# Linear attention and a gated convolution FFN on one core: unread matmuls at the start, k^T v copied between halves by DMA, and another written-out order

## The chip, the core and the metric

The kernel runs on one core of a Trainium2 chip. The metric is the device time in microseconds. An engine here is one of PE (matmul; PEld is its weight loads), DVE (vector), ACT (scalar, with its function tables), POOL and SP; each works through its own list of instructions in order and waits where an operand isn't ready. SP only issues DMAs here, POOL issues the loads and does a little arithmetic.

## The reference

Inputs are q, k, v of 8 batches, 8 heads, 576 positions and 64 columns, a gain of 64, and the FFN's weights. For each batch and head:

```
kv  = k^T v                                   # 64 x 64
o   = q kv                                    # 576 x 64
x   = o / sqrt(mean(o*o) + 1e-6) * g_norm     # heads side by side: 576 x 512
h   = relu(x w_in)                            # 576 x 1024
c   = conv over positions, 3 taps per column of h
out = (h * sigmoid(c)) w_out                  # 576 x 512, f32
```

## The kernel before

The eight batches go through in five groups: 0, 1, (2,3), (4,5), (6,7). Heads are handled in pairs; a pair is a t of 0 to 3, its two heads on partitions 0 to 63 and 64 to 127. The 576 positions are split in two halves of 288, called e.

For each batch, POOL loads k, v and q (line 239) as bf16, from f32 in DRAM; two buffers each. Batch 0 comes in two parts, of six and two heads. PE then does:

- kv_mm (line 380): k^T v. Group 0 (KV_TWICE 1) computes each product twice, so that it stands in both partition halves. The other groups compute it once, and kv_out (lines 386 to 397) copies each head's result into both halves, in four evictions of 64x256.
- tr_mm (line 430): transposes q through PE; tr_out evicts qT.
- out_mm (product, line 353): o from kv and qT, into a PSUM tile of two banks (a ring of three). ACT squares it (line 453), and for groups 0 to 2 "keep" stores it times g_norm in o32. Groups 3 and 4 ("dma") compute the product again later (out_again).
- ss_mm (line 507): sums of squares. ln_exp on ACT makes rs, the reciprocal root (lines 518, 519); group 4 uses a Newton iteration on POOL instead (lines 534 to 537).
- rs is then spread over partitions: by matmul (rb_mm, lines 624 and 627) in groups 0 to 2, after a split into bf16 parts on DVE from group 1 on; by DMA in groups 3 and 4. There "scatter" writes rs to DRAM (scr) and issues eight broadcast reads into rb (line 587), one entry in the order.
- x_mul or x_scale (lines 642, 648) on DVE gives xT.
- h_mm (line 746), eight matmuls for one f of 128 columns, and h_out with relu on ACT or DVE.
- The convolution: in group 0 on PE with diagonal weights (line 785), elsewhere on DVE: tap and add (lines 810, 831, 833). ACT does the sigmoid (lines 794, 837), DVE the gate (line 842).
- o_mm (line 698) with w_out, its eviction to o_sb (lines 333, 335; three buffers), and the store on SP (line 712). tails_mm takes the last 64 rows of two batches together.

A PSUM ring of two single banks serves k^T v, q's transposes, the sums and o_ps.

The order on all engines is written out: ORDER is a list of operation numbers, in which a letter a or d chooses ACT or DVE where both can do it, and "*n" puts n unread matmuls of 288 columns ("fill", line 343) ahead of that operation on PE, into the PSUM tile that it is about to write. The numbers count the plan.op calls. The costs, lat and dma figures given to plan.op are kept beside each operation and change nothing in the program: only ORDER and the data's own dependences do.

Of the kernel before, what the change touches and what calls it, by code (L numbers as in the profile page):

```python
# [25 lines left out]
def _patch_pnc_remap() -> None:  # L26
# [45 lines left out]
KV_TWICE = (1, 0, 0, 0, 0)  # L72
# [4 lines left out]
    0 105 11 104 8 10 12 1 2 7 17 18a 9 19 20d 29 30a 24 25d 26*5 27 21 22 6 34 35d 31 32 103 23a 36  # L77
    37d 41*7 28d 38*3 40d 33d 4 42 43*6 44 108 109d 39 49 45 46 5 50 3 13 118*9 123 124a 51 53 119a
    106 107a 54 204 47 110*5 111 113 114a 52 48 55 125 112d 56a 126 127d 14 203 202 68 69d 120 122d
    210 211d 121 220 115 116 59 117d 60d 128 129 130 57 58 77 64 207 215 65a 78a 73 74a 221d 131 132  # L80
    61 216d 62 225 226a 133 134 137 208 209a 138 206 135 82 136 83d 205 66 67 212 213 217 232 218
    364 214d 219d 233d 247 139 140a 222 224d 223 248d 227 237 238a 143 144a 242 243d 147 149 63 141
    75 228 142a 148 230 231d 362 79 229a 76 80 81 145 146a 363 15 234 249 250 236d 370 251a 70 239*4
    16 235 71 150 151 367 240 152 371d 153 155 86*3 87a 378 382 366 383d 244 245 156 365 72 379d 167
    252 168d 241d 253 254 374*2 375d 246a 84*3 85 163 164a 169 170a 88 165 154 89 255 157 158 166a
    171 90 259 256 368 369a 173 260 172 160 91 265 175 266 372 373 92d 93 267 268 174 376 377 388
    389a 384 385 396 397a 176 261*2 269 159 100 101a 161 179 516 515 270 262 177 257 386 380 97 387a
    381 390 392 258 178 283 180 393a 391 514 181 185 98d 400 401d 263 394 395 182 183 162 522 523d
    94 264 402 403 526 527d 184 519 398 271 399 95d 99 534 535a 520 521a 186 199 272d 284d 404 405
    285 286d 200a 277 273 278d 274d 287 275 276d 540 548 279 541a 290 549a 280d 518 281 552 528 282a  # L90
    529 517 536 537 538 539a 288 317 318a 309 313 314a 289 310a 291 292 294 293 96 311 312a 305 306a
    295 296 544 545a 550 551 303 304a 102 297 406 315 316a 307 308a 323 546 553d 554 555 547 319 321
    322 530 531a 190 191a 192 542 320 543 524 525 324 328 325 532 533 193 194a 407 408 409 410 556
    557 558 559 413 411 414 196 415 412 416 417 421 422 300 298 301 187 299 419 418 201 420 423 437
    424a 197a 438a 429 430a 431 425 432a 327 326 329 302 195 332 427 198 426a 439 428a 433 434a 441
    440 435 560 436a 442 443 444 445 447 446 331 333 461 462a 465 459 466a 448 460a 330 334 463 455
    456a 467 468a 469 188a 470a 457 458a 189 449 356 357a 358 464a 450 350 351a 352 453 359 360a 361
    563 561 573 471 474 473 341 342a 343 472 475 476 562 574 564 452 335 336a 344 345a 353 354a 480
    477 479 478 481 565 567 568 571 572 566 337 347 338 451 575 576 485 482 569 570 484 577 578a 454
    603 604a 483 486 585 579 580a 586 583 584a 588 607 629 348a 630a 581 582a 601 602a 587 346 511  # L100
    349 512a 608a 355 589 339a 590 591 592 593 605 606a 627 594 595 628a 599 597 625 609 663 496 631
    340 610 613 612 611 614 616 618 664a 598 626a 632a 617 490 497a 615 596 491a 513 498 619 622 620
    505 506a 507 600 633 634 492 636 635 649 651 508 652a 623 637 638 642 640 621 509a 510 641 502
    650a 503a 639 643 647 645 646 624 499 500a 672 690 653 654 644 655 504 501 691a 692 656 658 657
    659 673a 648 493 494a 495 487 665 666 660 667 668 669 661 488a 662 674 675 489 676 677 678 684
    685a 670 671 679 681 682a 687 686 680 693 683 688a 689 694d 695 705 706a 707 696 697d 698 699
    700d 701 702 703a 704
# [6 lines left out]
class Ring:  # L114


    def __init__(self, bufs):
        self.free = bufs
# [12 lines left out]
class Op:  # L131
# [4 lines left out]
    def __init__(self, at, group, engines, cost, fn, args, deps, need, lead, dma, lat):  # L136
        self.at, self.group, self.engines, self.cost = at, group, engines, cost
        self.fn, self.args, self.lead, self.dma, self.lat = fn, args, lead, dma, lat
        self.kind = fn.__name__ if fn else ""
        self.shape = SHAPE.get(self.kind, "")  # L140
        self.deps = sorted({d.at for d in deps})
        self.need = sorted({d.at for d in need})
        self.takes, self.gives = [], []
        self.engine, self.fill = engines[0], 0
# [7 lines left out]
class Plan:  # L152
# [8 lines left out]
    LOADED = 14.4  # L161
# [4 lines left out]
    def op(self, engines, cost, fn, *args, deps=(), need=(), lead=None, dma=0.0, lat=0.0):  # L166
# [3 lines left out]
               max(cost) if lead is None else lead, dma, lat)  # L170
# [20 lines left out]
def kernel(  # L191
# [37 lines left out]
    nc.scalar.preload_act_table_set(NORM_TABLES)  # L229

# [60 lines left out]
    nc.vector.tensor_copy(spread, spread_ps)  # L291

# [46 lines left out]
    def fill(op, ps):  # L339

        for _ in range(op.fill):
            n = min(ps.shape[-1], 288)
            nc.tensor.matmul(ps[:, :n], ident, spread.rearrange("p c m -> p (c m)")[:, :n],  # L343
# [690 lines left out]
```

## Time and profile before

The median of 13 runs is 206.15 us (205.03 to 208.11).

| | |
|---|---|
| profiled execution, its own time | 205.56 us |
| its span in the trace | 203.8 us |
| PE busy, of it fills | 184.0 us, 49 fills |
| DVE, ACT, POOL busy | 156.6, 139.2, 39.9 us |
| first v lands, first k^T v starts | 9.06, 9.19 us |
| first h_ps starts | 28.9 us |
| first h_ps of group 2 starts | 77.7 us |
| last k of batch 7 lands | 95.3 us |
| last matmul group starts | 197.5 us |

Times in the profile are microseconds from the start of the span, or nanoseconds where it says so. A line of groups gives source line, engine, operation, out<-in, shapes and count, then busy time and mean nanoseconds of one, then the idle time just before and what ended it. A window's line gives the stretch, its length and how long each engine was busy in it (with the number of instructions), then the granted clock, the DMA share and GB/s. The chain gives start, duration and what the time went to, from the last instruction back.

### The profile page before, as it was taken

The page shows a single profiled execution, that of the slowest core. Times are in us where ns is not written, and L with a number is a line of the kernel's source. Part 1 is how long each engine was busy: PE and PEld are TensorE (multiplying, and loading weights), DVE is VectorE, ACT ScalarE, POOL GpSimd, SP SyncE. Part 2 cuts the span into 40 slices and gives each one's busy share as a digit, 9 for nine tenths or more (in the row PEclk, how much of TensorE's full clock was granted, in tenths as well). Part 3 has the DMA queues.
Part 4 walks back from the last instruction along what each step waited for, and adds up shares of the span by engine and source line. Part 5 has one row for each costly group of instructions (what it writes and reads, how often), then busy time and mean ns, then how long its engine had stood idle before and what let it go on. Part 6 is the DMA issues. An engine that isn't in the chain of part 4 may idle for free.

```text
span 203.8 us, 4614 instructions
## 1 busy us (share of the span) xinstructions
PE 184.0 (90%) x1854; PEld 116.3 (57%) x1866; DVE 156.6 (77%) x289; ACT 139.2 (68%) x223; POOL 39.9 (20%) x61
## 2 busy tenths in 40 slices
PE   1299998998999999998999997896999999999991
PEld 0276665776677555776764575652448665554440
DVE  2145956768899898578979999999959999998320
ACT  2036364887889899856788969974598598686311
POOL 7706022070220503001000996000000000000000
PEclk9999999999999999999999999999999999999999
DMA  4999999999999499997994110897510341455554
GB/s 50 201 203 202 205 205 203 204 201 203 208 203 203 55 220 206 153 229 151 218 202 117 45 51 29 182 219 219 156 51 3 103 105 51 124 136 156 153 129 130
DMA packets 31593, 31.01 MB, mean 152 GB/s; under 512 B 2108, under 2 KB 26964, under 8 KB 31572
## 3 DMA queue, kind: packets, MB, share of 16 engines
q0 software_dynamic: 20976, 16.25, 52.5%
q1 hardware_dynamic: 10596, 14.47, 28.3%
q8 instruction: 14, 0.23, 0.5%
q14 instruction: 7, 0.06, 0.1%
HBM read 37.24 MB, written 9.73 MB: 230 GB/s over the span
## 4 chain that ended last, share of the span: by engine, by line
PE 52%; DMA 18%; issue 10%; POOL 9%; ACT 5%; DVE 4%; SPq 0%; POOLq 0%; ACTq 0%; DVEq 0%
PE o_ps L698 19%; PE h_ps L746 16%; DMA k_sb<-in_k_dram 7%; DMA out_dram<-o_sb 4%; PE kv_ps L380 3%; DMA v_sb<-in_v_dram 3%; PE qT_ps L430 3%; POOL rs L537 2%; PE rb_ps L624 2%; DMA rb<-scr 2%; PE c_ps L785 2%; ACT sq L453 2%; PE ot_ps L353 2%; DVE o L337 2%; PE ot_ps L343 1%
## 5 line engine op out<-in xcount | busy, mean ns | idle before, releaser
L746 PE MATMUL h_ps<-xT,w_in_sb 128*128 128x288 bf16 x512 | 67.4, 286 | 2.2 <-ACT h L757 1.8
L698 PE MATMUL o_ps<-w_out_sb,h 128*128 128x512 bf16 x260 | 60.3, 380 | 2.2 <-ACT o_sb L333 1.7
L746 PEld LDWEIGHTS <-w_in_sb 128*128 128x128 bf16 x512 | 48.9, 98 | 16.5 <-issue 2.9
L698 PEld LDWEIGHTS <-h 128*128 128x128 bf16 x272 | 25.7, 98 | 32.0 <-issue 3.3
L757 ACT ACTIVATE h<-h_ps 128x576 bf16<-128x576 f32 x53 | 33.3, 650 | 9.2 <-PE h_ps L746 8.7
L837 ACT ACTIVATE conv<-conv,cw_rel 128x576 bf16<-128x576 bf16 (+1 forms) x40 | 37.0, 960 | 1.8 <-DVE conv L833 1.6
L810 DVE TENSOR_SCALAR tap<-h,cw_rel 128x576 bf16<-128x576 bf16 (+1 forms) x80 | 31.4, 434 | 2.9 <-ACT h L757 2.1
L333 ACT ACTIVATE o_sb<-o_ps 128x512 f32<-128x512 f32 x30 | 17.8, 593 | 19.5 <-PE o_ps L698 10.3
L453 ACT ACTIVATE sq<-ot_ps 128x576 bf16<-128x576 f32 x32 | 20.1, 652 | 7.1 <-DVE o L337 4.1
L822 POOL COPY conv<-h 128x4 bf16<-128x4 bf16 (+3 forms) x12 | 3.3, 277 | 102.0 <-ACT h L757 71.6
L833 DVE TENSOR_TENSOR conv<-conv,tap 128x1152 bf16<-128x1152 bf16 (+11 forms) x36 | 21.9, 663 | 1.1
L842 DVE TENSOR_TENSOR h<-h,conv 128x1152 bf16<-128x1152 bf16 (+3 forms) x16 | 21.9, 1367 | 1.1 <-ACT conv L837 1.0
L831 DVE TENSOR_TENSOR conv<-h,tap 128x1152 bf16<-128x1152 bf16 (+11 forms) x36 | 20.4, 621 | 0.4
L333 ACT ACTIVATE kv_sb<-kv_ps 64x256 bf16<-64x256 f32 (+1 forms) x25 | 9.6, 382 | 12.4 <-PE kv_ps L380 12.1
L335 DVE COPY qT<-qT_ps 128x576 bf16<-128x576 bf16 x18 | 8.1, 452 | 8.7 <-PE qT_ps L430 8.7
L648 DVE SCALAR_TENSOR_TENSOR xT<-ot_ps,g_sb,rb 128x576 bf16<-128x576 f32 x16 | 12.2, 811 | 2.7 <-PE ot_ps L353 2.3
L239 POOL DMA_DIRECT2D q_sb<-in_q_dram x9 | 6.9, 768 | 35.8 <-PE qT_ps L430 25.2
L642 DVE TENSOR_TENSOR xT<-o,rb_ps 128x576 bf16<-128x576 f32 x15 | 11.0, 749 | 3.7 <-PE rb_ps L627 2.3
L353 PE MATMUL ot_ps<-qT,kv_sb 64*64 64x288 bf16 x192 | 12.9, 309 | 1.0 <-DVE o L337 0.4
L380 PE MATMUL kv_ps<-v_sb,k_sb 96*64 96x64 bf16 x432 | 10.2, 207 | 3.8 <-DMA v_sb<-in_v_dram 3.1
L430 PE MATMUL qT_ps<-ident,q_sb 96*128 96x96 bf16 x192 | 13.5, 215 | 0.0
L337 DVE TENSOR_SCALAR o<-ot_ps,g_sb 128x576 f32<-128x576 f32 x12 | 9.6, 812 | 5.1 <-ACT sq L453 4.1
(73 smaller groups left out, 161.4 us busy)
## 6 DMA issues: line engine op xcount, KB each, us to landing
out_dram<-o_sb SPq DMA_DIRECT2D x24, 192.0 KB, 2.4
rb<-scr SPq DMA_DIRECT2D x16, 288.0 KB, 6.1
q_sb<-in_q_dram POOLq DMA_DIRECT2D x7, 576.0 KB, 7.6
v_sb<-in_v_dram POOLq DMA_DIRECT2D x7, 576.0 KB, 11.7
k_sb<-in_k_dram POOLq DMA_DIRECT2D x7, 576.0 KB, 14.3
out_dram<-o_sb SPq DMA_DIRECT2D x24, 128.0 KB, 2.4
out_dram<-o_sb SPq DMA_DIRECT2D x24, 64.0 KB, 2.0
w_in_sb<-in_moe_w_in_dram POOLq DMA_DIRECT2D x2, 512.0 KB, 14.5
```

The source lines that it names most:

```text
L333: nc.scalar.activation(dst, src, AX.Copy, scale=1.0 if scale is None else scale)
L353: nc.tensor.matmul(ps[i * D:(i + 1) * D, e, :HS], g.kv[bi][es, t, i, :], g.qT[bi][es, 2 * t + i, :], start=True, stop=True)
L430: nc.tensor.transpose(ps[:, i, j * PS:(j + 1) * PS], q_sb[:, 2 * t + i, j * P:(j + 1) * P], ident[:PS, :PS])
L453: nc.scalar.activation(g.sq[bi, t], ust["ps"][:, :, :HS], AX.Square)
L698: nc.tensor.matmul(st["ps"][:n, :], g.h[:, f, t0:t0 + n], w_out_sb[:, f, :], start=(f == 0), stop=(f == n_ff - 1))
L746: nc.tensor.matmul(ps[:, e, :HS], w_in_sb[:, t, f * P:(f + 1) * P], g.xT[:, t, at:at + HS], start=(t == 0), stop=(t == n_hd - 1))
L757: nc.scalar.activation(dst, st["ps"][:, :, :HS], AX.Relu)
L810: eng.tensor_scalar_mul(cst["t"][:, f - f0, :], g.h[:, f, lo:lo + T], cw_rel[:, j, f:f + 1])
L831: nc.vector.tensor_add(c[:, :, here], h[:, :, here], t[:, :, there])
L833: nc.vector.tensor_add(c[:, :, there], c[:, :, there], t[:, :, here])
L837: nc.scalar.activation(cst["c"][:, f - f0, :], cst["c"][:, f - f0, :], AX.Sigmoid, scale=cw_rel[:, 1, f:f + 1])
L842: nc.vector.tensor_mul(hs, hs, cst["c"])
```

## The change

Five things change.

1. A tile of ones is set on DVE at the start, and PE runs 14 unread matmuls of it ahead of the transposes that make spread, and 22 after them. The fills ahead of single operations read ones too (instead of ident and spread), and there are 70 of them, not 49.
2. Groups 1 to 4 evict k^T v once, as 128x256, and kv_swap on SP copies it between the partition halves with two SBUF to SBUF DMAs of 32 KB. product reads slot 0 of kv for heads that are already in the right half and slot 1 for the swapped ones.
3. scatter is split: the write of scr, and four gathers of two broadcast reads each, which may stand apart in the order.
4. ORDER is another list: other positions on all engines, other choices of ACT and DVE, other loads first (v and k of batch 1, w_in, then q).
5. The planner's figures and its after and mates fields change (lat, LOADED); they act only through ORDER. tap can run on ACT by the code, but TAPS stays DVE.

The diff, without the list and the planner's figures:

```diff
-KV_TWICE = (1, 0, 0, 0, 0)
+KV_FROM = ("twice", "swap", "swap", "swap", "swap")
...
+    ones = consts.tile([P, 288], BF16, name="ones")
+    nc.vector.memset(ones, 1.0)
+    warm_ps = ps_one.tile([P, 288], FP32, name="warm_ps", tag="one")
+
+    def warm(n):
+        for _ in range(n):
+            nc.tensor.matmul(warm_ps, ones[:, :P], ones, start=True, stop=True)
+
+    warm(14)
...
     spread = consts.tile([P, 4, P], BF16, name="spread")
     nc.vector.tensor_copy(spread, spread_ps)
+    warm(22)
...
-            nc.tensor.matmul(ps[:, :n], ident, spread.rearrange("p c m -> p (c m)")[:, :n],
+            nc.tensor.matmul(ps[:, :n], ones[:, :P], ones[:, :n],
                              start=True, stop=True)
...
+                kv = (g.kv[bi][es, int(i != e), t, :] if g.kv_from == "swap"
+                      else g.kv[bi][es, t, i, :])
...
+                    if g.kv_from == "swap":
+                        g.kv[bi] = attn.tile([P, 2, n_hd, D], BF16, name="kv_sb", bufs=6)
+                        move(st["op"], g.kv[bi][:, 0, :, :], st["ps"][:, :, 0, :])
+                        return
...
+                def kv_swap(bi=bi):
+                    for i in range(2):
+                        nc.sync.dma_start(out=g.kv[bi][(1 - i) * D:(2 - i) * D, 1, :, :],
+                                          in_=g.kv[bi][i * D:(i + 1) * D, 0, :, :])
...
             def scatter():
-                scr = dram.tile([P, HS], FP32, name="scr")
-                nc.sync.dma_start(out=scr, in_=g.rs)
...
+                g.scr = dram.tile([P, HS], FP32, name="scr")
+                nc.sync.dma_start(out=g.scr, in_=g.rs)
+
+            def gather(t):
...
+                row = g.scr[t * SM:t * SM + 4 * g.G, :].rearrange("(c i) n -> i c n", i=2)
+                for i in range(2):
+                    nc.sync.dma_start(
+                        out=g.rb[i * D:(i + 1) * D, t, :, :],
+                        in_=row[i:i + 1].to_broadcast([D, 2 * g.G, HS]))
```

The start of the new order on PE reads, with the operations' names: k^T v of batch 0 (7 fills ahead), q's transposes t0 (8 fills) and t2, product t0, transposes t1, product t2, transposes t3 (3), product t1, k^T v of the last two heads, product t3 (3), sums, cw, rb t0 (6), sums (2), rb t2 (2), rb t1 (2), rb of t3's first half (2), k^T v of batch 1 (1), rb of t3's second half (1), h_mm f0 (1), f1, conv f0, h_mm f3, two transposes of batch 1. The first product of batch 1 follows conv f1. Group 1's and most of group 0's h_mm come ahead of q's transposes for group 2, where the old order mixed them.

## The prediction

> **What bounds it now.** I read the page's busy shares first, then the windows by stage, then the chain of waits in order of time. The first and second:
>
> ```profile
> PE 184.0 (90%) x1854; PEld 116.3 (57%) x1866; DVE 156.6 (77%) x289; ACT 139.2 (68%) x223; POOL 39.9 (20%) x61
> ...
> 28.90:67.30 38.40, 36.54 (x505) 26.84 (x501) 30.49 (x59) 30.20 (x50) 8.83 (x13) 1.00 1.29 202
> 67.30:77.70 10.40, 9.92 (x124) 4.95 (x122) 9.37 (x20) 9.22 (x18) 2.40 (x3) 1.00 0.92 147
> 110.00:142.80 32.80, 29.27 (x234) 18.32 (x230) 32.18 (x40) 25.84 (x34) 12.97 (x14) 1.00 0.54 129
> 142.80:197.50 54.70, 54.40 (x325) 29.76 (x331) 43.58 (x91) 38.11 (x58) 1.35 (x6) 1.00 0.39 107
> ```
>
> PE sets the time, but part of its 90% is no work: 49 filling matmuls, and at the start matmuls at half speed. From 142.8 us on PE has almost no gap. In 110 to 142.8 us DVE is busy 98% and PE stands 3.5 us. The chain shows the slow start and two later stalls:
>
> ```profile
> 2.23 6.82 DMA v_sb<-in_v_dram
> 9.06 0.14 issue
> 9.19 2.14 PE kv_ps L380 x72
> ...
> 13.11 1.20 PE ot_ps L343 x5
> ...
> 25.62 0.96 PE kv_ps L380 x48
> ...
> 27.75 0.72 PE ot_ps L343 x5
> ...
> 133.20 8.81 DMA out_dram<-o_sb
> 142.03 0.04 ACTq L333
> 142.07 0.05 issue
> 142.11 0.61 ACT o_sb L333
> ```
>
> The first k^T v takes 29.7 ns a matmul, the one at 25.62 us 20.0 ns; a fill takes 240 ns at 13.1 us, and 122 ns where fills stand among other warm work (288 columns; h_ps runs at 0.98 us for 8). The column of the granted clock says 1.00 all along, so the cold clock is read from durations alone. At 133 us a store lands 8.8 us later, behind the eight transfers that spread rs (rb<-scr), its o_sb comes free late, and PE stands 1.66 us at 141.1.
>
> Dividing each step's issue-to-issue time by its warm cost (h 0.99, o 1.73, product 0.25, transposes 0.26, k^T v 0.96 us), PE needs 169 us of own work and 6.0 us of fills after the first load (9.16 us); 15 us of waits and slow clock make up the rest up to the last o_ps at 197.5, and 6.3 us follow from its start on.
>
> **Part 1, warm matmuls and the first stage.** 14 fills start when ones is set, about 1.1 us (PE's first weight load stood at 1.26). At 240 ns they last to 4.5; the 16 transposes for spread need 0.6, then come 22 more. The rule in TensorE: Matmul & The Clock Gate, Part 1, is that some 3.4 us of sustained activity opens the clock, in a window that runs free of the kernel; that would open it at 4.5 to 8. The row here is slower: PE starts at 9.2 and reaches full speed only between 14.3 and 18, 5 to 9 us later, with gaps and transposes between. By the page the 22 end at about 8.2 and the 7 fills ahead of the first k^T v are over at the landing (9.06): nothing lost. By the row (open at 8) they end at 9.2 and the 7 at 10.1: 0.9 us lost. I take 0.5 late. If the clock didn't open at all, 22 + 7 at 240 ns would end at 12.1: 3 us lost.
>
> Walking the new order at warm costs: k^T v 9.6 to 11.0, 8 fills (1.0) to 12.0, transposes, first product 12.9 (before: 14.27). ACT then carries k^T v out 0.49, qT 0.65, three squares, keep 0.73 and the two rs steps 0.95, so the first rb_ps is at 17.1 (before: 19.63 after its fills). Four rb_ps pairs at 1.16 (one of them as two halves), 10 fills, and k^T v of batch 1 at 0.96 bring the first h_ps to 24.3 instead of 28.87. v and k of batch 1 are now loaded ahead of its q: k lands about 19.8 (now 22.75) and w_in 22.5 (now 25.3), so neither is late. Left over for afterwards are four transposes and one product of batch 1: 1.3 us. **-3.3 us.** The cover: diag (3 x 1.2 us on DVE) is now between the x steps; its last part ends at 25.7, and the first c_ps needs it at 26.3.
>
> **Part 2, k^T v by DMA.** Seven times, four evictions become one:
>
> ```profile
> L333 ACT ACTIVATE kv_sb<-kv_ps 64x256 bf16<-64x256 f32 x24 | 9.1, 378 | 3.1 <-PE kv_ps L380 2.7
> L335 DVE CAST kv_sb<-kv_ps 64x256 bf16<-64x256 f32 x4 | 1.7, 422 | 0.6 <-PE kv_ps L380 0.5
> L514 ACT ACT_TABLE_LOAD x2 | 2.6, 1283 | 0.0
> ```
>
> Of 28 pieces 7 stay: 10.8 us become about 2.7. ACT saves some 6.5, but the new order takes the sigmoid table before batch 1's rs and needs two more table loads (2.6), three more o_sb (1.8) and three more keeps (2.2): ACT stays as it is, DVE sheds 5. Neither sets the end, so this is worth nothing directly. What is added is a wait: kv_mm, eviction (0.39 and 0.2 of hops), then two DMAs of 32 KB on SP, then the product. PE work between a k^T v and its batch's first product in the new order: batch 1 5.8 us, batch 2 12.4, batch 3 6.0, batch 4 17, batch 5 9.3, batch 6 8.0, batch 7 5.3. The nearest rows of SP's transfers, with loads in flight (83 to 97 us) and without:
>
> ```profile
> out_dram<-o_sb SPq DMA_DIRECT2D x2, 128.0 KB, 6.9
> out_dram<-o_sb SPq DMA_DIRECT2D x1, 192.0 KB, 7.0
> scr<-rs SPq DMA_DIRECT2D x1, 144.0 KB, 5.2
> ...
> 125.26 1.75 DMA scr<-rs
> ```
>
> The rule in DMA: Bandwidth & Descriptors, Anatomy of one DMA, is a fixed 2.0 us plus bytes over 436 GB/s: an estimate of 2.1 us each, 3.4 with eviction, hops and the second issue (0.65), under every cover: 0 us. The same page (Issuing engines are not separate DMA queues) speaks against it, and the row agrees: under loads a 144 KB transfer took 5.2, not 1.75. By the rows 5.2 to 7.0 a swap is ready 6.4 to 8.2 after its k^T v: batch 1 loses 0.6 to 2.4, batch 3 0.4 to 2.2, batch 7 1.1 to 2.9, together 2.1 to 7.5. A swap moves under half of scr's bytes, so I take 4.5 us, and of what is late **+1.0 us**; ends 0 and 7.5. On SP the swaps stand between stores; batch 7's stands behind the scr write, which waits for rs on ACT that stands ahead of its own eviction there, so that costs one issue (0.6). Behind a swap on SP wait stores, which have time until three o_sb are full.
>
> **Part 3, the order in the middle (28.9 to 77.7 us).** The old order has 2.3 us of PE gaps there, 1.7 us of fills and some 2 of slow hand-overs. In the new one PE has 46 us of work, fills included, from the first h_ps (24.3) to the first h_ps of batches 2 and 3: 70.3 with no wait, 77.7 before. DVE has 43 us of work from 25.7 to the x steps that this needs: 68.4 if never idle, and it has idled a fifth of the time there. I put it at 72.5: with the 3.3 above, **-1.9 us** more (ends: -4 and +3).
>
> **Part 4, spread by quarters and the last third.** The gather of rb becomes four entries with stores between; the bytes and the 16 issues are the same. The store at 133 us then stands behind four transfers of 1.36 us each and not eight, and the fourth o_sb after it isn't needed before it lands: **-1.7 us** of the stall at 141. The other two stalls (1.15 and 0.62, PE waiting for ACT's h behind sigmoids) come from DVE, which is full there; from the first h_ps of batches 4 and 5 to the last x DVE has 32 us, PE 31. I take **-0.9**. Against it, 13 fills outside the first two stages (13 x 122 ns = 1.6), half of them in waits: **+0.8**. The last 10 us of PE are o_ps in both orders.
>
> **Sum.** -3.3 + 1.0 - 1.9 - 1.7 - 0.9 + 0.8 = -6.0. Span 203.8 becomes 197.8. The profiled run took 205.56, 1.76 more than its span, and stands 0.6 under the median of 206.15; with both, 200.2 us; I say **200.5**.
>
> **Rivals.** (a) DVE paces the middle: the first stage's 3.3 us are waited off before batch 2's x steps, because DVE, 98% full at 110 to 142.8, is no sooner there; only the o_sb stall goes. For it: DVE's share; against: DVE sheds 5 us. 204.0. (b) The swap is the new wait, and slower than before: batches 1, 3 and 7 have 5.3 to 6.0 us of cover. At 9.0 us each from k^T v to landing (the longest rb<-scr row) they lose 3.2, 3.0 and 3.7, and batch 6 1.0; from there each later product is late too and the ring of three product tiles stops PE: 11 us where the sum has 1, so 210.5. It decides from about 7.9 us on, where the three losses reach the 6.6 us that all else gains. (c) The warming doesn't do what it says: the clock is still closed at 9 us and the fills hold up the first k^T v by 3 us. Then the first stage gains 0.5: 203.3. (d) The order holds as walked, with no late swap, and DVE never idle: 196.5.
>
> **Numbers.** The forecast (198 to 203) 0.58, (d) 0.10, (a) 0.13, (c) 0.07, (b) 0.12. A time within 0.5% (1 us) counts as the same, about what a measurement of this kernel can tell. Of (a) and (c) about a third falls within it, so faster 0.81, same 0.06, slower 0.13. The range runs from (d) to just over no change, leaving out (b) and little else: 196.5 to 206.5.
>
> **What would show it.** First k^T v near 20 ns a matmul and begun by 9.7 us; first h_ps at 24 to 25 us; first h_ps of batches 2 and 3 at 71 to 74; products of batches 1, 3 and 7 not waiting for a kv_sb DMA over 1 us; swaps landing in 3 to 5.5 us; no ACT wait for out_dram over 1 us. Wrong if fills at 240 ns end after 10 us, if swaps take over 7 us, or if DVE's idle share in the middle stays as it is.

## The result, and the profile after

The changed kernel took 204.26 us (median of 11 executions, 200.91 to 213.2), the kernel before 206.41 us beside it (48 executions). The ratio, which leaves out executions over 1.5% above the fastest of their kernel, is 0.987, 95% interval [0.983, 0.991]: faster by 1.3%. I had said 200.5 us, 2.7% faster, with a range from 196.5 to 206.5. The direction and the range held; of the 5.7 us foretold, some 2 came in the median.

The profiled execution is another matter. Its own time is 200.76 us and its span 199.0, against 205.56 and 203.8 before: -4.8 us, where my sum says -6.0. The two differ because of the granted clock, the share of its full speed that PE is given: 1.00 is full, 0.5 is half, and an execution's figure is the mean. Of twelve executions of the changed kernel two had a mean granted clock of 1.00 (spans 199.0 and 199.1), nine had 0.972 to 0.980 (201.8 to 203.9), one 0.94 (211.4). The profile has a record of each change of this clock; until the first record its column reads 1.00 even where PE runs at half speed, so the slow start of the kernel before doesn't show in it. Most of the executions of the kernel before that ran beside the experiments had 0.987 or more.

The same views as before, of the profiled execution at clock 1.00. The busy shares, one group and one transfer of the page (line numbers are those of the new kernel: h_ps 784, o_ps 736, product 370, swap 422, evictions 348 and 350, taps and sums 852 to 874):

```profile
PE 188.9 (95%) x1911; PEld 119.2 (60%) x1923; DVE 151.5 (76%) x282; ACT 136.0 (68%) x210; POOL 39.9 (20%) x61
...
L348 ACT ACTIVATE kv_sb<-kv_ps 128x256 bf16<-128x256 f32 (+2 forms) x8 | 3.1, 382 | 14.1 <-PE kv_ps L396 14.1
...
kv_sb<-kv_sb SPq DMA_DIRECT2D x14, 32.0 KB, 5.2
```

The 28 pieces of k^T v have become single evictions, and the 14 swap DMAs land 5.2 us after issue. The windows, cut at the first h_ps, at the first h_ps of group 2 and at the ends of the stage from 110 to 142.8 us:

```profile
25.04:75.66 50.62, 48.76 (x638) 33.77 (x640) 42.53 (x86) 40.29 (x64) 10.87 (x17) 1.00 1.21 193
75.66:110.00 34.34, 34.20 (x445) 22.96 (x449) 28.64 (x47) 26.65 (x44) 3.55 (x6) 1.00 1.03 183
110.00:142.80 32.80, 31.81 (x235) 19.67 (x236) 32.03 (x41) 24.92 (x34) 13.22 (x14) 1.00 0.60 158
```

PE has 1.9 us of gaps in 50.6 us of middle, and in 110 to 142.8 its gaps went from 3.5 to 1.0 us. The chain of the changed kernel:

```profile
2.22 6.99 DMA v_sb<-in_v_dram
9.25 1.33 PE kv_ps L396 x72
...
17.04 1.23 PE rb_ps L659 x4
...
25.34 1.96 PE h_ps L784 x16
...
54.44 1.51 DVE conv L872 x3
55.97 1.62 DVE tap L852 x4
57.68 1.50 DVE conv L874 x3
...
75.73 1.09 PE h_ps L784 x8
```

The first k^T v now runs at 18.5 ns a matmul (1.33 us for 72) and begins when v lands; the store that landed after 8.8 us is gone from the chain; new in it is DVE's convolution of group 1.

By stage, start of the first real matmul of each, in the kernel before and after, both at clock 1.00:

| | before | after | gained so far |
|---|---|---|---|
| first k^T v | 9.19 | 9.25 | 0 |
| first h_ps | 28.91 | 25.18 | 3.7, with 1.3 us of batch 1's work left for later |
| first h_ps of group 2 | 77.75 | 75.67 | 2.1 |
| end of the span | 203.8 | 199.0 | 4.8 |

So the front gives about 2.4 net, the middle loses 0.3 of it, and from the first h_ps of group 2 on the kernel gains 2.7.

### The profile page after: what moved, and what is told of

The parts are those of the page before. It is cut to its first block, busy times and chain, and to the rows that moved or that the text cites. A ratio compares the mean times of both kernels' runs of the same rounds, so it can differ in the third digit from the quotient of the medians.

```text
span 199.0 us, 4723 instructions
## 1 busy us (share of the span) xinstructions
PE 188.9 (95%) x1911; PEld 119.2 (60%) x1923; DVE 151.5 (76%) x282; ACT 136.0 (68%) x210; POOL 39.9 (20%) x61
## 3 DMA queue, kind: packets, MB, share of 16 engines
q1 hardware_dynamic: 11716, 14.93, 29.1%
## 4 chain that ended last, share of the span: by engine, by line
PE 69%; DVE 20%; issue 4%; DMA 4%; ACT 1%; POOL 0%; DVEq 0%; ACTq 0%; POOLq 0%
PE h_ps L784 22%; PE o_ps L736 22%; DVE tap L852 7%; DVE conv L872 4%; PE ot_ps L370 4%; PE qT_ps L459 4%; DVE conv L874 4%; DMA v_sb<-in_v_dram 4%; PE kv_ps L396 3%; PE rb_ps L659 2%; PE c_ps L824 2%; DVE xT L683 2%; PE o_ps L927 2%; PE qT_ps L358 2%; PE ot_ps L358 2%
## 5 line engine op out<-in xcount | busy, mean ns | idle before, releaser
L795 ACT ACTIVATE h<-h_ps 128x576 bf16<-128x576 f32 x52 | 32.7, 650 | 17.5 <-PE h_ps L784 16.5
L736 PEld LDWEIGHTS <-h 128*128 128x128 bf16 x272 | 25.9, 98 | 30.1 <-issue 1.4
L348 ACT ACTIVATE o_sb<-o_ps 128x512 f32<-128x512 f32 x33 | 19.7, 597 | 16.4 <-PE o_ps L736 9.1
L883 DVE TENSOR_TENSOR h<-h,conv 128x1152 bf16<-128x1152 bf16 (+3 forms) x16 | 22.5, 1407 | 0.1
L863 POOL COPY conv<-h 128x4 bf16<-128x4 bf16 (+3 forms) x12 | 3.3, 276 | 95.8 <-ACT h L795 54.2
L874 DVE TENSOR_TENSOR conv<-conv,tap 128x1152 bf16<-128x1152 bf16 (+11 forms) x36 | 20.4, 622 | 1.1
L797 DVE TENSOR_SCALAR h<-h_ps 128x576 bf16<-128x576 f32 x12 | 9.1, 754 | 5.5 <-PE h_ps L784 5.4
L459 PE MATMUL qT_ps<-ident,q_sb 96*128 96x96 bf16 x192 | 12.7, 206 | 0.0
L348 ACT ACTIVATE kv_sb<-kv_ps 128x256 bf16<-128x256 f32 (+2 forms) x8 | 3.1, 382 | 14.1 <-PE kv_ps L396 14.1
L459 PEld LDWEIGHTS <-q_sb 96*128 96x128 bf16 x192 | 10.5, 97 | 2.9 <-issue 1.4
```

The costliest lines, as they stand in the source:

```text
L348: nc.scalar.activation(dst, src, AX.Copy, scale=1.0 if scale is None else scale)
L459: nc.tensor.transpose(ps[:, i, j * PS:(j + 1) * PS], q_sb[:, 2 * t + i, j * P:(j + 1) * P], ident[:PS, :PS])
L736: nc.tensor.matmul(st["ps"][:n, :], g.h[:, f, t0:t0 + n], w_out_sb[:, f, :], start=(f == 0), stop=(f == n_ff - 1))
L795: nc.scalar.activation(dst, st["ps"][:, :, :HS], AX.Relu)
L874: nc.vector.tensor_add(c[:, :, there], c[:, :, there], t[:, :, here])
L883: nc.vector.tensor_mul(hs, hs, cst["c"])
```

## The experiments

### What the warm matmuls are worth, and the granted clock

The first set: the changed kernel once more, the same without its warm matmuls, and the kernel before with nothing but the warm matmuls added.

**The changed kernel again**, no edit.

> The changed kernel as it is, run again to see the granted clock of each execution. Theory A (the clock falls back): the warm matmuls open PE's clock at about 4.7 us, and in most executions it closes again for some 8 us while little runs on PE in the first stage, so that mean granted clock is 0.975 to 0.98 and the span 201.8 to 203; the others read 1.00 and 199.0 to 199.3. Theory B (density): the clock drops late, because the new order leaves PE no gaps. Theory C (chance, any kernel): the kernel before shows the same spread.

Measured: median 204.83 us (6 executions); spans and clocks 211.0 at 0.94, 203.6 at 0.972, 204.0 at 0.979, 199.0 at 1.00, 202.5 at 0.98, 202.0 at 0.979. The kernel before beside it had 207.47 us. The page's rows of clock and PE in 40 slices of 5.3 us, of the execution at 0.94:

```profile
PE   7969999999999898999999989999999999999990
...
PEclk9995555899999999999999999999999999999998
```

PE is busy through all of the half-speed stretch. By the recorded changes of the granted clock it opened at 4.8 us, closed at 15.0 and opened again at 38.9. In that execution q's second part landed at 14.97 us and not 13.61, and PE stood 1.4 us for it just before the clock closed. So the clock does fall back, as Theory A says; that all kernels show it alike (Theory C) doesn't fit, since 14 of 17 executions of the kernel before had 0.989 or more.

**Without the warm matmuls.**

> The changed kernel without its 14 and 22 unread matmuls at the start (the fills stay). Theory A: every execution opens the clock once, between 12 and 18 us, mean granted clock (counted from the first opening) 1.00 in all, spans within 1 us of each other, at 201.5 to 203. Theory B: 0.975 to 0.98 in most, as with the warm matmuls, and about 2 us slower than the changed kernel. Theory C: as B.

```diff
-    warm(14)
...
-    warm(22)
```

Measured: 207.16 us (6 executions). One execution had clock 1.00 and a span of 200.7 us; the others 203.7 to 205.4 at 0.973 to 0.98. So the warm matmuls are worth 1.7 us where the clock stays open (200.7, a single execution, against 199.0), but taking them away did not take away the closing: it moved. Two windows of the profiled execution (0.974):

```profile
14.00:24.20 10.20, 10.01 (x97) 5.54 (x95) 6.13 (x10) 6.21 (x12) 1.55 (x2) 1.00 1.30 205
24.20:34.40 10.20, 10.20 (x80) 6.23 (x81) 3.91 (x6) 2.32 (x3) 2.29 (x3) 0.50 1.30 205
```

The clock opened at 13.9 us, was closed from 24.2 to 34.4, and PE had no idle time worth the name ahead of it. So it closes without the little work on PE that Theory A gave as the reason, though not late, as Theory B had it.

**Warm matmuls alone, in the old order.**

> The kernel before with only the 14 and 22 unread matmuls added. My step says that the warm clock is worth 0.65 us in the first k^T v and some 2 us up to the first rb_ps: 1.5 to 2.5 us off in an execution whose clock stays open. Theory A: in most executions the clock falls back, mean 0.97 to 0.98, and the gain is 0.5 us or less in the median. Theory B: the clock reads 1.00 in all, since the old order is not denser: 204.0.

```diff
+    ones = consts.tile([P, 288], BF16, name="ones")
+    nc.vector.memset(ones, 1.0)
...
+    warm(14)
...
+    warm(22)
```

Measured: 203.53 us (6 executions), ratio 0.986 [0.979, 0.993]. Spans 201.0 to 202.3 at 0.987 to 1.00, one 205.1 at 0.983. At clock 1.00 the old order with warm matmuls has a span of 201.0, 2.8 us under the kernel before. So this one edit gives in the median as much as the whole change gives (0.986 and 0.987): the old order mostly keeps the clock open and the new one mostly does not. The profiles say more: with the warm matmuls the old order has its first h_ps of group 2 at 75.68 us, the changed kernel at 75.67. Up to there the other edits add nothing to the warm matmuls, although the new order has its first h_ps 1.7 us earlier (25.18 against 26.84); the 2.0 us from 201.0 to 199.0 come behind that point.

Where does it close? The recorded changes lie on a grid of 3.41 us: every closed stretch ahead of the last matmuls is 3.41, 6.83, 10.24, 13.65, 23.89 or 27.31 us long. Between the first rb_ps and the first h_ps stand sixteen f32 matmuls of 32 rows, 290 ns each on average, in groups of two or four. Counting the matmuls that start in one full window of that stretch, the one ahead of the closing where there is one (fills are the unread matmuls; the names of later runs are marked):

| kernel | window, us | fills | rb_ps f32 | other | clock in the next window |
|---|---|---|---|---|---|
| before | 20.46 to 23.87 | 9 | 5 | 9 transposes, 2 sums | open |
| before, warm | 19.51 to 22.92 | 9 | 6 | 12 transposes | open |
| after, at 1.00 | 18.36 to 21.77 | 4 | 8 | 2 sums | open |
| with four evictions (below) | 18.61 to 22.02 | 6 | 8 | none | half |
| without late fills (below) | 19.85 to 23.27 | 5 | 8 | none | half |
| without warm | 20.75 to 24.17 | 5 | 9 | none | half |
| all gathers moved (below) | 18.44 to 21.85 | 5 | 8 | 2 sums | half |
| less DVE work (below) | 18.96 to 22.37 | 7 | 8 | none | open |
| ten more fills (below) | 20.30 to 23.71 | 8 | 7 | none | open |
| 15 fewer fills (below) | 16.95 to 20.36 | 2 | 12 | 2 sums | half |

The new order loads k and v of batch 1 ahead of its q, so batch 1's transposes no longer stand between the rb_ps; what is left there is f32 matmuls and few fills. The changed kernel stayed open with 4 fills in this trace where others closed with 5 or 6, so the counts alone don't decide it near the edge. Hence three edits of the fills alone: more of them there, fewer there, and none behind this stretch.

**Ten more fills between the first rb_ps and the first h_ps.**

> The changed kernel with ten more fills where f32 spread matmuls follow each other (rb t2, t1, t3's first half 4 each in place of 2, k^T v of batch 1 and rb of t3's second half 3 in place of 1). Theory D (the stretch of f32 spread matmuls counts as little PE activity and lets the clock close at about 22 us; fills hold it open): mean granted clock 0.995 to 1.00 in most executions, span 199.0 + 10 x 0.122 = 200.2, own time 202, 2.5 us under the changed kernel's median. Theory E (the clock closes whatever is between, by chance): 0.98 as before and 1.2 us slower.

```diff
-    42 39 43*6 49*2 47*2 105 33a 45*2 50 44 4 46 51*2 52 106*1 107a 48 53*1
+    42 39 43*6 49*2 47*4 105 33a 45*4 50 44 4 46 51*4 52 106*3 107a 48 53*3
```

Measured: 202.31 us (6 executions, 201.81 to 203.52), ratio 0.980 [0.975, 0.985]. All six had a clock of 0.997 to 1.00 and spans of 200.0 to 201.7. The page's clock row has no slice under 9; the windows on the grid of that execution:

```profile
16.90:20.30 3.40, 3.33 (x19) 1.68 (x17) 2.88 (x5) 2.48 (x6) 0.25 (x1) 1.00 1.28 208
20.30:23.70 3.40, 3.40 (x17) 1.88 (x16) 1.00 (x2) 0.11 (x1) 0.00 (x0) 1.00 1.30 203
23.70:27.10 3.40, 3.40 (x62) 2.03 (x62) 1.52 (x4) 0.39 (x1) 1.21 (x2) 1.00 1.26 205
```

The middle one holds 8 fills and 7 rb_ps, and the clock stayed open. Ten matmuls that do nothing cost 1.2 us where the clock would have stayed open anyway (200.6 against 199.0; the other 0.4 us come from the first k^T v, at 9.68 in place of 9.25: in this execution the clock opened at 6.64 and not at 4.71, and the fills ahead of it lasted beyond v's landing at 8.95), and where it would not they save 1.2 to 3.3 (200.6 against 201.8 to 203.9). This version is faster than both kernels in the median; against the kernel before its ratio is 0.980 where the changed kernel has 0.987, with intervals that overlap a little.

**Fifteen fewer fills there.** Six ahead of the first rb_ps and nine between it and the first h_ps go; the two ahead of the sums stay.

> The changed kernel without any fill from the first rb_ps to the first h_ps (16 fewer). Theory D: the clock closes in every execution, about one window earlier (18 to 22 us), 3 or more windows of 3.4 us, span 203 to 206. Theory E: mean clock 0.98 or 1.00 as before, and up to 1.9 us faster for the fills left out.

```diff
-    42 39 43*6 49*2 47*2 105 33a 45*2 50 44 4 46 51*2 52 106*1 107a 48 53*1
-    54 3 55*1
+    42 39 43 49*2 47 105 33a 45 50 44 4 46 51 52 106 107a 48 53
+    54 3 55
```

Measured: 202.48 us (6 executions), ratio 0.979 [0.974, 0.984]; clock 0.971 to 0.979 in all six, spans 199.4 to 203.0. The clock closes every time, in the profiled one from 20.36 to 27.19 us after a window of 12 rb_ps and 2 fills in which PE also stood 0.6 us. The closing was as expected, its length (two windows, not three or more) and the time were not: I had given 203 to 206. The fifteen fills (not sixteen, as I had counted) are 1.8 us of PE time at 122 ns each, and the closed stretch is 6.8 us here, and 10.2 in the profiled executions without warm matmuls and with four evictions. So in the median the amount of fills in the changed kernel is the worst of the three: it pays for them and mostly loses the clock all the same.

**None of the 32 fills behind the first h_ps.**

> The changed kernel without the 32 fills behind the first h_ps. My step put 13 of them at +0.8 us and the others in waits. If the clock needs none of them: 0.5 to 1.5 us faster than the changed kernel at the same granted clock. If it does: it closes at 58 to 70 us or at 98 to 104 us too, and 2 to 4 us slower.

```diff
-    102 367 94 95d 96 226a 219*1 235*1 236d 250*1 251d
+    102 367 94 95d 96 226a 219 235 236d 250 251d
...
```

Measured: 204.44 us (6 executions), ratio 0.985 [0.978, 0.991]; four executions at 0.960 to 0.966 (202.6 to 204.0), two at 0.983 (199.7 and 200.0). The page's clock row of one of the four:

```profile
PEclk9999759999998899999987999999999999999998
```

Three closings: 23.3 to 30.1 in the f32 stretch, as in the others, and two of 3.4 us each, at 64.2 and 105.2 us, each behind a place where fills were taken out and PE stood 1.3 and 0.9 us of the last window. The later fills do hold the clock, and cost about what they save: 32 fills are 3.9 us, and the two closings are 3.4 us at most.

### The swap

**Four evictions again in the new order.**

> The changed kernel with the copies between halves done by four evictions again in place of one and two DMAs; the order stays. My step: nothing directly; the eviction of 1.58 us in place of 0.39 is under every cover, so 0 to +1 us against the changed kernel. Rival: the relief of ACT (7 x 1.2 us) is what the order was worth, and it is 2 to 4 us slower. Rival: the swaps make PE wait, and it is 0.5 to 1 us faster.

```diff
-                        move(st["op"], g.kv[bi][:, 0, :, :], st["ps"][:, :, 0, :])
+                        for slot in range(2):
+                            for half in range(2):
+                                i = half ^ slot
+                                move(st["op"], g.kv[bi][half * D:(half + 1) * D, slot, :, :],
+                                     st["ps"][i * D:(i + 1) * D, :, 0, :])
```

Measured: 207.0 us (12 executions), ratio 1.001 [0.997, 1.006]: all that the change gains is gone, as the rival with 2 to 4 us had it. But its clock was never 1.00 (0.969 to 0.983, twice 0.944), so the same edit was also made on the version with ten more fills.

**Four evictions with the clock held open.**

> The changed kernel with ten more fills between the first rb_ps and the first h_ps (its span was 200.0 to 200.6 us with the granted clock at 1.00), and k^T v again moved by four evictions in place of one eviction and two DMAs; the order of instructions stays. The clock now being open in both, the swap is compared without it. My prediction (the DMA swap is worth nothing directly, 0 to +1 us): span 200 to 201. Rival (the three ACT or DVE moves per batch that the swap spares are on the path, since DVE paces 46 to 60 us and ACT is 95% busy there): +2 to +2.5, span 202 to 203, most of it in the first h_ps of group 2 (77.3 without the change).

The edit is that of the run before, with the fills of the version with ten more.

Measured: 204.41 us (10 executions), ratio 0.992 [0.989, 0.995]; nine executions at 0.994 to 1.00 with spans of 202.1 to 203.7, against 200.0 to 201.7 with the swap. (In the tenth, 215.7 us at 0.937, q's second part landed at 14.93 us and the clock closed at 15.0, as in the execution at 0.94 above.) So the swap is worth about 2 us with the clock open (median spans 202.5 and 200.6). Where? Three stretches of the first version with four evictions, behind its closing, and of the changed kernel, from the first h_ps of group 1 to that of group 2, from there to that of group 3, and to the end; the clock is 1.00 in all of them. First four evictions, then the swap:

```profile
47.07:81.31 34.24, 31.83 (x424) 20.76 (x425) 29.57 (x66) 28.81 (x49) 7.60 (x12) 1.00 0.98 160
81.31:120.67 39.36, 37.31 (x474) 24.54 (x474) 31.94 (x52) 33.28 (x56) 6.90 (x11) 1.00 0.90 168
120.67:205.68 85.01, 79.97 (x505) 46.55 (x511) 66.35 (x118) 57.18 (x86) 11.41 (x15) 1.00 0.45 120
```

```profile
42.68:75.67 32.99, 31.60 (x424) 20.68 (x425) 28.11 (x63) 27.66 (x46) 7.60 (x12) 1.00 1.16 187
75.67:113.51 37.84, 37.14 (x474) 24.31 (x474) 31.83 (x52) 30.15 (x47) 6.57 (x11) 1.00 1.01 191
113.51:198.99 85.48, 79.99 (x505) 46.49 (x511) 66.97 (x118) 57.06 (x86) 11.60 (x16) 1.00 0.45 120
```

1.25 and 1.5 us, and nothing (-0.5) later. In both stretches PE has the same work to a few tenths, and its gaps grow from 1.4 to 2.4 and from 0.7 to 2.1 us; ACT has 1.2 and 3.1 us more. ACT is not full in either (84 to 85% with four evictions). PE's waits with four evictions:

```profile
PE ot_ps L358 <- ACT sq L484: 0.8, 1, 0.8
PE ss_ps L539 <- ACT sq L484: 0.7, 1, 0.7
PE o_ps L738 <- ACT rs L550: 0.6, 1, 0.6
...
PE qT_ps L358 <- ACT qT L348: 0.5, 1, 0.5
```

These four are 2.6 us; the changed kernel has one wait for ACT, of 0.2 us for a square. So PE waits for squares, rs and qT from an ACT that has the extra evictions in its list too. That these pieces stand right behind them is my reading; the waits show only which engine PE waited for.

**The swap in the old order**, with the warm matmuls, each swap straight behind its eviction and the gathers straight behind their scr write.

> The order of instructions of the kernel before, with the warm matmuls and with the swap by DMA put straight behind each eviction of k^T v, and the gathers straight behind their scr write. The old order with the warm matmuls and the four evictions had a span of 201.0 us at clock 1.00. If the swap is worth 2 us by what it takes off ACT in any order: 199 to 200. If it needs the new order, which leaves 5 us between the eviction and the first product: the products wait for it, 2 to 4 us in group 1 (first product of batch 1 due at 26.3 us) and again in the later groups, span 203 to 208.

```diff
-    9 11 8 10 7 12 17*7 18a 19*8 20d 104 103 29 30a 21 22 24 25d 31 32 23d 36*3 26 27 37d 34 0 35a
...
+    0 105 11 104 8 10 12 1 2 7 17 18a 9 19 20d 29 30a 24
...
+    51 53 120a 106 107a 108 54 205 47 111*5 112 114 115a 52 48 55 126 113d
...
```

(106 to 108 are k^T v of batch 1, its eviction and its swap; 111 is its first product.) Measured: 224.56 us (6 executions), ratio 1.088 [1.082, 1.094]: 21 us slower than the old order with four evictions and the warm matmuls. PE's waits:

```profile
PE ot_ps L379 <- DMA kv_sb<-kv_sb: 11.3, 7, 4.1
PE ot_ps L379 <- DVE xT L692: 4.3, 2, 3.9
```

Seven waits for swaps, 4.1 us the longest. The clock closed five times between 11.4 and 137.7 us, 23.9 us in all, which can cost PE up to half of that. I had not counted with that part, and 203 to 208 was far too little. The swap has its 2 us only in an order that puts other PE work between a k^T v and its products.

### What sets the middle

The chain of the changed kernel goes through DVE at 47.5 to 59.8 us, and my rival (a), which I gave 0.13, said that DVE paces the middle. So the version with ten more fills had a part of DVE's work taken out there: the second taps and two thirds of the second sum of group 1's convolution.

> The changed kernel with the ten more fills, and in group 1 alone the second set of eight taps and two of three parts of the second conv sum left out (the conv of that group is then not the reference's), which takes about 5.3 us of VectorE work out of 46 to 60 us. If VectorE paces the middle (the rival that I gave 0.12): first h_ps of group 2 earlier by 2 to 4 us (from 77.3 to 73.5 to 75.3). If TensorE paces it, as my Part 3 took: within 0.5 of 77.3.

```diff
                 def tap(j, f=f, f0=f0, nf=nf, cst=cst):
+                    if g.n == 1 and j == 2:
+                        return
...
-                for at, n, prev in ((HS, HS, 0), (PS, HS - PS, HS), (1, PS - 1, S - PS)):
+                for at, n, prev in ((HS, HS, 0), (PS, HS - PS, HS), (1, PS - 1, S - PS))[:1 if g.n == j == 1 else 3]:
```

Measured: span 199.9 us in the profile, median 202.36. The stretch from 44 to 61 us, first with all of DVE's work and then with the part left out:

```profile
44.00:61.00 17.00, 16.65 (x196) 12.07 (x196) 14.87 (x41) 15.20 (x27) 5.01 (x8) 1.00 0.93 141
```

```profile
44.00:61.00 17.00, 16.87 (x204) 12.27 (x203) 11.56 (x29) 15.58 (x28) 4.91 (x8) 1.00 0.98 149
```

DVE does 3.3 us less here, and PE was full already. The first h_ps of group 2 starts 50.0 us after the first h_ps (26.15 to 76.16) in place of 50.4 (26.81 to 77.18): 0.4 us for 3.3 us of DVE work. (76.16 is 1.0 us earlier than 77.18, outside both expectations, but 0.7 of that was there at the first h_ps, ahead of the part left out.) DVE doesn't pace the middle, PE does, to within these 0.4 us; the chain ran through DVE because of one wait of PE for it, 0.6 us at 59.2. A place in the chain says who came last, not by how much.

### The gathers

**All gathers of groups 3 and 4 straight behind their scr write.**

> The changed kernel with the four gathers of each group straight behind the scr write on SP, as in the kernel before. My step: the stores behind them land late again, ACT waits for an o_sb for 2 us or so at 135 to 142 us, and PE stands 1 to 1.7 us. Rival: the new order of o_ps alone avoids it, and nothing changes (within 0.5 us at the same granted clock).

```diff
-    548 410 549a 300 411 550 320 321d 540 541d 308 309d 322 324 325 202 302 412 551 415 552a 414 310
+    531 298 297 545d 376 377 306 307a 93 312 313a 409 548 410 549a 300 411 412
+    415 414 413 550 320 321d 540 541d 308 309d 322 324 325 202 302 551 552a 310
...
-    476 477a 468 467a 469a 480 481 350 351a 483 472 473a 474 475a 484 571 482 485 487 489 486 488
-    490 459 344 199 572 575 352 573 345a 346 353 354a 355 460 461 338 339a 341 342a 576 577 578 582
-    574 343 359 360a 361 340 462 347 491 583 580 494 586 579 362 363a 492 587 581 590 588 589 591
+    476 477a 468 467a 469a 480 481 350 351a 483 472 473a 474 475a 484 571 572 575
+    573 574 482 485 487 489 486 488 490 459 344 199 352 345a 346 353 354a 355
...
```

(411 and 571 are the scr writes, 412 to 415 and 572 to 575 the gathers, 550 batch 7's swap.) Measured: 221.11 us (6 executions), ratio 1.068 [1.063, 1.073], far off every expectation. The edit moved more than I meant: in SP's list the gathers of group 3 now stand ahead of batch 7's swap. SP's timeline, and PE's wait:

```profile
99.66 0.35 SPq L620 DMA_DIRECT2D scr<-rs  x1
101.48 5.73 SPq L628 DMA_DIRECT2D rb<-scr  x8
107.31 1.22 SPq L431 DMA_DIRECT2D kv_sb<-kv_sb  x2
```

```profile
PE ot_ps L379 <- DMA kv_sb<-kv_sb: 9.2, 1, 9.2
PE o_ps L745 <- ACT o_sb L357: 3.9, 2, 3.5
```

The swap is issued at 107.3 us and not at 95.8 (4.3 us of this were there at the scr write already, 99.66 against 95.36, since in this execution the clock had closed in the f32 stretch), PE stands 9.2 us, the clock closes at 107.2 for 13.7 us, and group 4's Newton steps on POOL begin at 126.6 and not at 110.2. The edit costs 17 us in the median, but not all for the swap: the 3.5 us that PE waits for an o_sb come with group 4's gathers, which the next run moves alone. For one swap of two 32 KB copies behind eight issues of 0.7 us that leaves some 13 us (an estimate: 17 less 3.5).

**Group 4's gathers alone**, on the version with ten more fills, so that no swap stands behind them.

> The changed kernel with the ten more fills, and the eight rb gathers of the last group alone put straight behind their scr write on SP, ahead of the output stores; those of the group before stay where they are, behind the swap. My Part 4 (the stores held behind the gathers stall o_sb and with it PE by 1.7 us, the other two stalls 0.9): a wait of PE for o_sb of 1.5 to 3.5 us near 130 to 145, span 201.5 to 203.5. Rival (DVE's gated convolution paces 112 to 142, so a stall of PE there is covered): the stall shows but the span stays at 200 to 201.

```diff
-    476 477a 468 467a 469a 480 481 350 351a 483 472 473a 474 475a 484 571 482 485
-    487 489 486 488 490 459 344 199 572 575 352 573 345a 346 353 354a 355 460
-    461 338 339a 341 342a 576 577 578 582 574 343 359 360a 361 340 462 347 491
+    476 477a 468 467a 469a 480 481 350 351a 483 472 473a 474 475a 484 571 572 575
+    573 574 482 485 487 489 486 488 490 459 344 199 352 345a 346 353 354a 355
+    460 461 338 339a 341 342a 576 577 578 582 343 359 360a 361 340 462 347 491
```

Measured: 206.72 us (12 executions), ratio 1.003 [0.998, 1.007]; three executions at clock 1.00 with spans of 203.8, 203.9 and 204.9 against 200.0 to 201.7. So about 3.5 us at the same clock. SP's timeline and the waits of PE and of ACT:

```profile
126.46 5.38 SPq L628 DMA_DIRECT2D rb<-scr  x8
131.94 20.47 SPq L759 DMA_DIRECT2D out_dram<-o_sb  x16
```

```profile
PE o_ps L745 <- ACT o_sb L357: 3.8, 1, 3.8
```

```profile
ACT o_sb L357 <- DMA out_dram<-o_sb: 6.8, 2, 5.8
```

The stores stand behind eight transfers, o_sb stays taken for up to 5.8 us, and PE stands 3.8 us at 137.2. Nearly its full length shows in the end; that DVE is 98% busy from 112 to 142 us, with and without the stall, covers little of it. In the profiled execution (0.988) the clock also closed for 3.4 us behind the stall, at 141.9; nine of the twelve were below 1.00, and in the median the edit costs 4.4 us.

## Why the prediction was right or wrong

**Part 1, the front: mechanism right, 0.9 us short, and the clock's premise wrong.** The warm matmuls opened the clock at 4.7 us in the profile of the changed kernel, and at 4.5 to 6.7 in the other traces that have them; the range that I worked out from the Trainium skill's page TensorE: Matmul & The Clock Gate, Part 1 (4.5 to 8), holds. Nothing was late in this profile, so the 0.5 us that I had allowed did not come; where the clock opened at 6.6 or 6.7 they did, with the first k^T v at 9.7. Here k^T v began at 9.25, the first rb_ps at 17.04 (17.1 foretold), but the first h_ps at 25.2 and not 24.3: in the walk I gave the stretch between 7.2 us, and it took 8.1. The walk has ten fills where the order has eleven, and each step from fills to f32 matmuls or k^T v and back lost 0.1 to 0.2 us that I had put at nothing. What failed is a premise that I didn't write out: that the clock, once open, stays open. The same section says that the clock falls back after an idle window of some 3.4 us. The traces differ from it: in the version with four evictions it closed at 22.0 us after a window in which PE was busy 3.40 of 3.40 us (the row stands at the end). By the page's rule nothing in that window closes the clock; by the granted clock of the executions, 15 of the 18 of the changed kernel lost it.

**The step to the median failed.** I carried the profiled execution's 0.6 us over to the median of the new kernel, as the old one has it. The old kernel's other executions stand near its profile because its order keeps the clock; the new one's profile is one of the two in twelve at 1.00, and its median stands 3.5 us above it. This is the larger part of the miss: 204.26 - 200.76 = 3.5, less the 0.6 allowed, against 1.2 us by which the sum misses the profiled execution. No term and no end of my range stood for the clock closing, so that the median still fell inside the range is luck. That holding the clock in the f32 stretch closes this gap is shown (six of six executions at 0.997 or more with ten fills); in the changed kernel itself I have no trace of an execution at 0.979, so that its clock closes at the same place as in the versions without warm matmuls, with four evictions and without late fills is inferred, not shown.

**Part 2, the swap: wrong in both terms.** Its landing (5.2 us, 4.5 taken) was near, the wait was 0.2 us in all and not 1.0. My estimate of 2.1 us a swap was out of place: the section Anatomy of one DMA of the Trainium skill's page DMA: Bandwidth & Descriptors gives its sum for DMAs that POOL issues, and SP issues the swaps; beside the loads they took 5.1 to 5.9 us. "Worth nothing directly" was wrong: about 2 us with the clock held open. I had looked at the totals of ACT (as before; 139.2 became 136.0 us) and DVE (5 us less, as came) and at neither's single pieces; with the evictions put back PE waits 2.6 us for ACT, which is only 84 to 85% busy. Rival (b), a swap that stops PE, did not occur here, but the old order with the swap (21 us, clock closings included) and the gathers ahead of a swap (some 13 of 17 us) show what such waits cost.

**Part 3, the middle: wrong.** I put the first h_ps of group 2 at 72.5; it came at 75.7. From the first h_ps I allowed 46 us of PE work and 2.2 us of gaps; it was 50.5. Step by step, with fills, PE's work at its warm cost is 46.1; 4.6 us are lost from 25.04 to 75.66. PE is idle for 1.9 of them, mostly at three waits:

```profile
PE qT_ps L358 <- DVE o_sb L350: 0.6, 1, 0.6
...
PE ss_ps L537 <- DVE qT L350: 0.5, 1, 0.5
...
PE ot_ps L370 <- ACT sq L482: 0.2, 1, 0.2
```

The other 2.7 go in the changes from one kind of matmul to another. So the work was sized right and the losses at less than half: "with no wait" isn't a sum of warm costs. One of my signs of being wrong came near: DVE was idle for 18% of the old middle (28.9 to 77.7 us) and is idle for 16% of the new one. Rival (a), DVE as the pace, gave 204.0, close to the median, but for a reason that the run with less DVE work refutes.

**Part 4, gathers and stalls: right in kind, too small.** The o_sb stall is gone, and ACT's longest wait for a store is 1.1 us. Undone in the new order, the stall costs about 3.5 us and not the 1.7 of the old trace; why it is larger there no run tells apart. PE's gaps in 110 to 142.8 fell by 2.5 us; I had taken 2.6 for the three stalls together. From the first h_ps of group 2 to the end -2.7 was measured, -1.8 foretold.

**The sum at clock 1.00:** the front gave 2.4 of 3.3 (0.9 short); the middle with its swap waits was to give 0.9 and lost 0.3 (1.2 short); the end gave 2.7 of 1.8 (0.9 better): -4.8 and not -6.0. That the end's surplus is as large as what the front lacks is chance. Two figures of the working are off or not shown, and neither is in the sum: 25.7 and 43 us make 68.7, not 68.4, and how the 196.5 of (d) adds up is not shown.

## What to carry to other kernels

A profiled execution tells what a kernel can do, not what it mostly does: read the mean granted clock of every execution before a sum is carried over to the median. When an order pulls dense work out of a stretch of small f32 matmuls, ask what keeps the clock open there; here ten unread matmuls more, or fifteen fewer, were both better than the number that only paid for them. A DMA that takes the place of evictions is worth it where other work lies between it and its reader, and then every entry that SP has ahead of it counts.

## What the runs showed of the hardware that I had not expected

- The granted clock closed while PE was busy 3.40 of 3.40 us. A window of the version with four evictions and of the changed kernel, just before the closing in the first and none in the second:

```profile
18.60:22.00 3.40, 3.40 (x16) 1.67 (x14) 1.49 (x3) 0.93 (x2) 0.00 (x0) 1.00 1.26 206
```

```profile
18.40:21.80 3.40, 3.40 (x16) 1.67 (x14) 1.80 (x2) 0.93 (x2) 0.00 (x0) 1.00 1.26 206
```

  By these rows nothing tells them apart: 16 matmuls each, 8 of them f32. The stretch is near the edge of closing, and where it falls on the 3.41 us grid differs from one trace to the next. With 7 or 8 fills to 8 or 7 f32 matmuls it stayed open (three traces), with 4 to 6 fills to 8 or 9 it closed in four of five, with 2 to 12 it closed. Whether the 32 rows or the f32 type is what counts was not tried.
- It also closed after windows in which PE stood for part of the time only: 0.9 and 1.3 us of 3.4 without the late fills, and 2.0 us in the old order with the swap, at 11.4 us.
- A closing in the f32 stretch or ahead of it lasted 6.8 to 27.3 us, but for one of 3.4 us in the old order with the swap, and matmuls take about twice as long in it: sixteen matmuls of h_ps took 4.05 us with four evictions and 2.12 in the changed kernel's profile.
- It opens 3.3 to 5.5 us after unread matmuls begin: at 4.5 to 6.7 us where they start at about 1.2, against 17.05 us in the kernel before, whose k^T v and transposes began at 9.2.
- A swap of 32 KB within SBUF took 5.1 to 5.9 us from issue to landing beside the loads (batches 1 to 5), 3.9 us for batch 6, and 1.8 and 3.1 us for batch 7, after the last loads. Behind the eight gathers batch 7's took 7.4 and 6.9 us.
